# Linear attention in a DiT block: KV per head on 32-column tiles, and KV folded into wo on 32x32 tiles

## The chip, the cores and the metric

The kernel runs on one core of a Trainium2 chip. The metric is the time of one execution on the device in microseconds (us), lower is better. A kernel is timed in several runs beside runs of the kernel before on the same chip. Ratios in this document are the mean time of one kernel's fast runs over the mean time of the other's fast runs of the same rounds, so they are not quite the ratios of the medians that are quoted.

TensorE is the matmul engine. Here a matmul of 128x128 weights with a 128x512 moving operand starts 0.216 us after the one before it. "PE" is TensorE in the profile, "PEld" its weight loads, DVE is VectorE, ACT is ScalarE, POOL is GpSimd, SP issues most DMAs.

## The reference, cut to what matters

```python
h   = layernorm(x) * (1 + ca) + sa                 # x: 2048 x 1024 bf16
q, k, v = split(h @ wqkv)                          # 32 heads of 32 columns
pq, pk  = phi(q), phi(k)
kv  = einsum('bhsd,bhse->bhde', pk, v)             # one 32x32 matrix per head
z   = sum over s of pk
o   = (pq @ kv) / (pq @ z + 1e-6)
x   = x + ga * (o @ wo)
h   = layernorm(x) * (1 + cb) + sb
x   = x + gb * ((silu(h @ w_gate) * (h @ w_up)) @ w_down)     # 3584 wide
```

## The kernel before

The sequence is cut into four chunks (`sc`) of 512 rows. K, V and later Q of a chunk are computed, and `kv_phase` adds the chunk's part to `kv_acc`. At the end KV is folded into `wo`, so that attention costs one matmul with `pq` (`a_ps`). Then the FFN runs per chunk: `gate_up(0), down(0), gate_up(1), down(1), ...`. The `wo_tile` work of the next chunk runs inside `down`.

```python
VW = P + 2
k8 = ctx.enter_context(tc.tile_pool(name="k8", bufs=19))      # 19 buffers of about 8 KB per partition
...
def big(name, shape):                       # every large tile takes one of the 19
    return k8.tile([P] + shape, BF16, name=name, tag="k8")
...
kvs = k8.tile([P, HG * VW + HG * P], F32, name="kvs", tag="k8")
kv_acc = kvs[:, 0:HG * VW].rearrange("p (g e) -> p g e", e=VW)
kvb = kvs[:, HG * VW:].bitcast(BF16).rearrange("p (k g e) -> p k g e", k=2, e=P)
KVZ, KVT = kvb[:, 0], kvb[:, 1]
...
def kv_phase(sc):                           # four heads at once: 128x128, three quarters of it wasted
    for hg0 in range(0, HG, 3):
        nh = min(3, HG - hg0)
        kvp = acc_b("kvp")
        kvv = kvp[:, 0:3 * (P + 1)].rearrange("p (g e) -> p g e", e=P + 1)
        for i in range(nh):
            for t in range(STC):
                mm(kvv[:, i, :], lhsT=pks[sc][:, t, (hg0 + i) * P:(hg0 + i + 1) * P],
                   rhs=vs[sc][:, t, hg0 + i, 0:P + 1], start=(t == 0), stop=(t == STC - 1))
        ... # copied or added to kv_acc on VectorE
...
# after the last chunk: off-diagonal heads are masked away, KV is transposed and folded into wo
KVZ = kv_acc * kvmask                                    # (cut) two VectorE instructions
for hg in range(HG):
    transpose(tpk[:, hg, :], KVZ[:, hg, :])
...
for hg, nb in wf[3 * (qc - 5):3 * (qc - 4)]:             # 16 of these, between Q steps
    mm(ps[:], lhsT=KVT[:, hg, :], rhs=w, start=True, stop=True)
    nc.scalar.copy(out=w, in_=ps[:])
...
def gate_up(sc, between=None):
    for fb in range(NFB):                                # 7 blocks
        for view in (wg_v, wu_v):
            w = big("wgu", [DC, FBW])                    # 1 MB of w_gate, 1 MB of w_up
            nc.sync.dma_start(out=w[:], in_=view[:, :, fb * FBW:(fb + 1) * FBW])
        for fj in range(FPB):                            # 4 groups of 8 gate and 8 up matmuls
            if f % GPT == 0:
                guT[sc].append(big("gu", [min(GPT, FC - f), SCW]))
            ...
```

## Time and profile before

| | before |
|---|---|
| median | 847.77 us (847.76 to 847.96, 3 runs) |
| PE busy | 99% of a span of 846.2 us |
| granted clock of TensorE | 0.999 |

From the page of the kernel before: busy time and share of each engine, then the busy share of TensorE and its granted clock in 40 equal slices (9 is 90% or more).

```profile
PE 838.6 (99%) x4284; PEld 385.7 (46%) x4284; DVE 307.2 (36%) x602; ACT 173.8 (21%) x267; POOL 55.7 (7%) x160
PE   8999999999999999999999999999999999999997
PEclk9999999999999999999999999999999999999999
```

TensorE never waits for long, and its granted clock is 0.999. Whatever is to change the time has to take work from TensorE, or to make it wait.

The chain of waits of the kernel before, in order of time (start in us, length in us, what, number of instructions):

```profile
16.30 5.35 PE acc L98 x24
...
65.16 1.81 PE kvp L98 x32
...
163.92 0.45 PE tp L101 x8
...
168.48 0.65 PE wf L98 x3
...
184.64 14.50 PE a_ps L98 x64
...
289.09 33.78 PE acc L98 x156
322.87 3.45 PE a_ps L98 x16
...
354.81 126.91 PE acc L98 x588
```

A KV phase (`kvp`) costs 1.81 to 1.82 us, four times, and the eight transposes (`tp`) 0.45 us. The fold (`wf`) runs between Q projections: five pieces of three matmuls at 0.65 us and a last one of 0.22 us. The two long `acc` pieces hold `gate_up` and the first matmuls of `down`: no wait interrupts them.

The weights of the FFN come over the SP queue. Three of its DMA issues from the timeline of SP:

```profile
315.13 0.37 SPq L614 DMA_DIRECT2D wd<-in_B_w_down_dram  x1
446.35 0.37 SPq L551 DMA_DIRECT2D wgu<-in_B_w_gate_dram  x1
448.08 0.37 SPq L551 DMA_DIRECT2D wgu<-in_B_w_up_dram  x1
```

These are not free choices of the queue. In `gate_up(1)` the issues are 13.81 us apart in two series, and 13.81 us is one block of 64 matmuls. One series falls on the last use of a block's gate weights, the other, 1.73 us later, on the last use of its up weights. Each load waits for a k8 buffer, and buffers are handed on in program order.

At the start, masks are built on POOL. This is the POOL timeline from 7.5 to 11.5 us:

```profile
8.29 0.31 POOL L181 MEMSET zmask<- 128x256 bf16 x1
8.54 0.58 POOL L184 MEMSET kvmask<- 32x32 bf16 x4
9.15 1.70 POOL L186 MEMSET zmask<- 32x1 bf16 x32
10.94 0.55 POOL L193 TENSOR_TENSOR rstd<-veps,neg_half 128x1 f32<-128x1 f32 x1
```

The third `rstd` could have run at 9.55 us, when its input was ready. It waits behind the memsets.

### The profile page before, as it was taken

How to read it: one execution, taken by the hardware profiler on the slowest of the kernel's cores; microseconds unless marked ns; L12 is line 12 of the kernel's file. 1: busy time of each engine (PE TensorE's matmuls, PEld its weight loads, DVE VectorE, ACT ScalarE, POOL GpSimd, SP SyncE). 2: the span in 40 equal slices, each digit the busy share in tenths (PEclk: the TensorE clock that was granted, in tenths of full speed). 3: DMA queues.
4: the chain of work that ended last, by engine and by line, in shares of the span. 5: the costliest groups of instructions: out<-in, count | busy, mean ns of one | idle time of the engine just before them, and what ended most of it. 6: DMA issues, size and time to landing. Idle time of an engine off the chain costs nothing.

```text
span 846.2 us, 10498 instructions
## 1 busy us (share of the span) xinstructions
PE 838.6 (99%) x4284; PEld 385.7 (46%) x4284; DVE 307.2 (36%) x602; ACT 173.8 (21%) x267; POOL 55.7 (7%) x160
## 2 busy tenths in 40 slices
PE   8999999999999999999999999999999999999997
PEld 4445445544444444444444444444444444444443
DVE  5756464467423325431111344211114431111121
ACT  1455453354311110101111010011110101111000
POOL 2101010012011001100000010000001100000000
PEclk9999999999999999999999999999999999999999
DMA  9893870029976765528434073581604639710011
GB/s 309 301 257 98 243 187 1 1 52 215 348 210 207 214 186 174 181 69 266 146 104 149 19 236 95 159 283 54 199 1 126 185 69 318 240 59 0 19 57 50
DMA packets 125840, 128.74 MB, mean 152 GB/s; under 512 B 33376, under 2 KB 107360, under 8 KB 125280
## 3 DMA queue, kind: packets, MB, share of 16 engines
q1 hardware_dynamic: 122208, 115.36, 46.0%
q0 software_dynamic: 3584, 12.72, 5.0%
q8 instruction: 33, 0.54, 0.3%
q14 instruction: 15, 0.12, 0.0%
HBM read 108.01 MB, written 12.71 MB: 143 GB/s over the span
## 4 chain that ended last, share of the span: by engine, by line
PE 98%; DVE 1%; POOL 0%; DMA 0%; issue 0%; ACT 0%; SPq 0%; DVEq 0%; POOLq 0%
PE acc L98 88%; PE a_ps L98 7%; PE kvp L98 1%; PE modr L98 0%; PE wf L98 0%; DMA x_sb<-in_A_x_dram 0%; DVE stats L199 0%; PE mod_ps L98 0%; PE den L98 0%; POOL zmask L186 0%; PE tp L101 0%; POOL rstd L193 0%; PE bcr L98 0%; DVE e L583 0%; DVE ob L585 0%
## 5 line engine op out<-in xcount | busy, mean ns | idle before, releaser
L98 PE MATMUL acc<-h2T,wgu 128*128 128x512 bf16 x1792 | 387.9, 379 | 0.0
L98 PEld LDWEIGHTS <-wgu 128*128 128x128 bf16 x1792 | 175.1, 98 | 211.0
L98 PE MATMUL acc<-wd,gu 128*128 128x512 bf16 x896 | 196.0, 379 | 0.0
L566 DVE TENSOR_TENSOR gu<-acc,e 128x512 bf16<-128x512 f32 x112 | 77.4, 691 | 300.4 <-PE acc L98 300.4
L565 ACT ACTIVATE e<-acc 128x512 f32<-128x512 f32 x112 | 66.9, 597 | 375.2 <-PE acc L98 375.2
L98 PEld LDWEIGHTS <-gu 128*128 128x128 bf16 x896 | 87.6, 98 | 105.8
L98 PEld LDWEIGHTS <-hT 128*128 128x128 bf16 x512 | 49.6, 98 | 60.8 <-DVE hT L212 1.0
L583 DVE TENSOR_TENSOR e<-acc,gb_bc 128x512 f32<-128x512 f32 x32 | 22.1, 691 | 130.5 <-PE acc L98 130.5
L98 PE MATMUL a_ps<-wo,pq 128*128 128x512 bf16 x256 | 57.9, 379 | 0.6 <-DVE pq L395 0.6
L98 PE MATMUL acc<-hT,wq 128*128 128x512 bf16 x256 | 57.1, 379 | 0.0
L98 PE MATMUL acc<-wk,hT 128*128 128x512 bf16 x256 | 56.9, 379 | 0.0
L98 PE MATMUL acc<-wv,hT 128*128 128x512 bf16 x256 | 55.9, 379 | 0.0
L263 ACT ACTIVATE eb<-acc 128x512 bf16<-128x512 f32 x64 | 37.9, 596 | 62.8 <-PE acc L98 60.5
L209 ACT ACTIVATE xn<-x,nmr,rstd 128x1024 bf16<-128x1024 f32 x16 | 19.8, 1240 | 127.6 <-POOL nmr L207 127.6
L264 DVE TENSOR_SCALAR eb<-eb 128x512 bf16<-128x512 bf16 x64 | 18.4, 291 | 60.6 <-ACT eb L263 60.6
L98 PEld LDWEIGHTS <-pq 128*128 128x128 bf16 x256 | 24.7, 98 | 31.8 <-DVE pq L395 2.6
L98 PEld LDWEIGHTS <-wq 128*128 128x128 bf16 x256 | 24.9, 98 | 29.8
L534 POOL DMA_DIRECT2D x_scratch<-x x16 | 9.6, 600 | 369.6 <-DVE x L527 369.6
L527 DVE TENSOR_TENSOR x<-a_ps,x_sb 128x512 f32<-128x512 f32 x32 | 22.1, 691 | 8.0 <-PE a_ps L98 7.9
L193 POOL TENSOR_TENSOR rstd<-veps,neg_half 128x1 f32<-128x1 f32 x32 | 18.2, 569 | 81.3 <-DVE veps L191 70.4
L301 ACT CAST v<-acc 128x512 bf16<-128x512 f32 x32 | 18.3, 582 | 22.1 <-PE acc L98 22.1
L528 DVE BATCH_NORM_STATS2 stats<-x 128x6 f32<-128x512 f32 x32 | 22.2, 695 | 1.1
(72 smaller groups left out, 280.7 us busy)
## 6 DMA issues: line engine op xcount, KB each, us to landing
wgu<-in_B_w_gate_dram SPq DMA_DIRECT2D x28, 1024.0 KB, 7.4
wgu<-in_B_w_up_dram SPq DMA_DIRECT2D x28, 1024.0 KB, 8.7
x_sb<-in_A_x_dram SPq DMA_DIRECT2D x32, 256.0 KB, 5.9
wml<-in_w_mod_dram SPq DMA_DIRECT2D x8, 1024.0 KB, 8.6
x_scratch<-x POOLq DMA_DIRECT2D x16, 512.0 KB, 3.1
x1r<-x_scratch SPq DMA_DIRECT2D x32, 256.0 KB, 3.0
wd<-in_B_w_down_dram SPq DMA_DIRECT2D x7, 1024.0 KB, 7.7
wme<-in_w_mod_dram SPq DMA_DIRECT2D x4, 1024.0 KB, 11.2
```

What stands on the lines that cost most here:

```text
L98: return tc.keep_in_program_order(nc.tensor.matmul(out, lhsT=lhsT, rhs=rhs, start=start, stop=stop))
L193: nc.gpsimd.tensor_tensor(out=rstd[:, 0:n], in0=veps[:, 0:n], in1=neg_half[:].to_broadcast([P, n]), op=ALU.pow)
L209: nc.scalar.activation(out=dst, in_=src, func=ACT.Identity, bias=nmr[:], scale=rstd[:, 0:1])
L263: nc.scalar.activation(out=e[:], in_=acc, func=ACT.Exp)
L264: nc.vector.tensor_scalar(out=e[:], in0=e[:], scalar1=1.0, scalar2=PHI_EPS, op0=ALU.min, op1=ALU.add)
L301: nc.scalar.copy(out=v[:, t, nb * 4:(nb + 1) * 4, 0:P], in_=acc[:].rearrange("p (g e) -> p g e", e=P))
L527: nc.vector.tensor_tensor(out=x1[:, ns], in0=a_ps[:], in1=x_t[:, ns], op=ALU.add)
L528: nc.vector.bn_stats(out=stats[:, nb, :], in_=x1[:, ns])
L534: nc.gpsimd.dma_start(out=x1_dram[st * P:(st + 1) * P, :], in_=x1[:])
L565: nc.scalar.activation(out=sg[:], in_=ps[0][:], func=ACT.Silu)
L566: gm = nc.vector.tensor_tensor(out=guT[sc][f // GPT][:, f % GPT, :], in0=ps[1][:], in1=sg[:], op=ALU.mult)
L583: nc.vector.tensor_tensor(out=yt[:], in0=y_ps[:], in1=gb_bc[:, ns], op=ALU.mult)
```

## The change

The intent is to stop computing the three quarters of each 128x128 KV product that the head mask throws away. Each head gets its own 32-column tile of the array, four heads side by side, all in one bank of PSUM, the memory that the matmuls of this kernel write to. KV is then compact, so there is no mask; two transposes do in place of eight; the fold runs on sixteen 32x32 tiles, for which the rows of `wo` are regrouped on load. The compact `kv_acc`, `KVB` and `KVT` move to the constant pool, and the k8 pool goes from 19 to 18 buffers.

```diff
-    VW = P + 2
+    VW = HPC * (DH + 1)
-    wo_v = A_wo.rearrange("(c p) n -> p c n", p=P)
+    wo_v = A_wo.rearrange("(h g i e) n -> h g e i n", h=2, g=4, i=HPC)
-    k8 = ctx.enter_context(tc.tile_pool(name="k8", bufs=19))
+    k8 = ctx.enter_context(tc.tile_pool(name="k8", bufs=18))
-    kvs = k8.tile([P, HG * VW + HG * P], F32, name="kvs", tag="k8")
-    ...
+    kv_acc = const.tile([P, HG, DH + 1], F32, name="kv_acc")
+    KVB = const.tile([P, HG, DH], BF16, name="KVB")
+    KVT = const.tile([P, 2, P], BF16, name="KVT")
 ... (kvmask and its memsets go; V is laid out as 33 columns per head, the last one 1.0)
     def kv_phase(sc):
+        W = DH + 1
+        kvp = acc_b("kvp")
+        for hg in range(HG):
+            for t in range(STC):
+                for i in range(HPC):
+                    mm(kvp[i * DH:(i + 1) * DH, hg * W:(hg + 1) * W],
+                       lhsT=pks[sc][:, t, hg * P + i * DH:hg * P + (i + 1) * DH],
+                       rhs=vs[sc][:, t, hg, i * W:(i + 1) * W], start=(t == 0), stop=(t == STC - 1))
 ... (wo is loaded by 8 DMAs of 32 partitions in place of 2 of 128)
+    def fold_wo(h, nb):
+        ns = slice(nb * NB, (nb + 1) * NB)
+        ps = [acc_b("wf") for _ in range(4)]
+        for i in range(HPC):
+            for g in range(4):
+                rs = slice(g * DH, (g + 1) * DH)
+                mm(ps[g][i * DH:(i + 1) * DH, :], lhsT=KVT[rs, h, i * DH:(i + 1) * DH], rhs=wo[h][rs, i, ns],
+                   start=True, stop=True)
+        for g in range(4):
+            (nc.scalar.copy if g % 2 == 0 else nc.vector.tensor_copy)(out=wo[h][:, g, ns], in_=ps[g][:])
+    q_phase(1, 4, 6)
+    fold_wo(0, 0)
+    q_phase(1, 6, 8)
+    fold_wo(0, 1)
+    q_phase(2, 0, 2)
+    fold_wo(1, 0)
+    q_phase(2, 2, 3)
+    fold_wo(1, 1)
```

More of the change, by code (lines that the diff above doesn't have):

```diff
@@ L169 @@
     gb_bc = const.tile([P, D], BF16, name="gb_bc")
-    kvs = k8.tile([P, HG * VW + HG * P], F32, name="kvs", tag="k8")
-    kv_acc = kvs[:, 0:HG * VW].rearrange("p (g e) -> p g e", e=VW)
-    kvb = kvs[:, HG * VW:].bitcast(BF16).rearrange("p (k g e) -> p k g e", k=2, e=P)
-    KVZ, KVT = kvb[:, 0], kvb[:, 1]
+    kv_acc = const.tile([P, HG, DH + 1], F32, name="kv_acc")
+    KVB = const.tile([P, HG, DH], BF16, name="KVB")
+    KVT = const.tile([P, 2, P], BF16, name="KVT")
     Zden = const.tile([P, HG, DH], BF16, name="Zden")
-    kvmask = const.tile([P, P], BF16, name="kvmask")
     zmask = const.tile([P, HG, DH], BF16, name="zmask")
@@ L179, in build_masks @@
     def build_masks():
-        nc.gpsimd.memset(kvmask[:], 0.0)
         nc.gpsimd.memset(zmask[:], 0.0)
@@ L183, in build_masks @@
             rs = slice(h * DH, (h + 1) * DH)
-            nc.gpsimd.memset(kvmask[rs, rs], 1.0)
             for hg in range(HG):
@@ L292, in v_phase @@
         vs[sc] = v
-        nc.gpsimd.memset(v[:, :, :, P:VW], 1.0)
+        vh = v.rearrange("p t g (i e) -> p t (g i) e", e=DH + 1)
+        nc.gpsimd.memset(vh[:, :, :, DH:DH + 1], 1.0)
         for t in range(STC):
@@ L300, in v_phase @@
                                      start=(cc == 0), stop=(cc == DC - 1))
-                nc.scalar.copy(out=v[:, t, nb * 4:(nb + 1) * 4, 0:P], in_=acc[:].rearrange("p (g e) -> p g e", e=P))
+                nc.scalar.copy(out=vh[:, t, nb * 16:(nb + 1) * 16, 0:DH], in_=acc[:].rearrange("p (h e) -> p h e", e=DH))
     def q_phase(sc, lo=0, hi=DC):
@@ L313, in kv_phase @@
     def kv_phase(sc):
-        for hg0 in range(0, HG, 3):
-            nh = min(3, HG - hg0)
-            kvp = acc_b("kvp")
-            kvv = kvp[:, 0:3 * (P + 1)].rearrange("p (g e) -> p g e", e=P + 1)
-            for i in range(nh):
-                for t in range(STC):
-                    mm(kvv[:, i, :], lhsT=pks[sc][:, t, (hg0 + i) * P:(hg0 + i + 1) * P],
-                                     rhs=vs[sc][:, t, hg0 + i, 0:P + 1], start=(t == 0), stop=(t == STC - 1))
-            dst = kv_acc[:, hg0:hg0 + nh, 0:P + 1]
-            if sc == 0:
-                nc.vector.tensor_copy(out=dst, in_=kvv[:, 0:nh, :])
-            else:
-                nc.vector.tensor_tensor(out=dst, in0=dst, in1=kvv[:, 0:nh, :], op=ALU.add)
+        W = DH + 1
[6 more added lines that the diff above has]
+                       rhs=vs[sc][:, t, hg, i * W:(i + 1) * W], start=(t == 0), stop=(t == STC - 1))
+        kvv = kvp[:, 0:HG * W].rearrange("p (g e) -> p g e", e=W)
+        if sc == 0:
+            nc.vector.tensor_copy(out=kv_acc[:], in_=kvv)
+        else:
+            nc.vector.tensor_tensor(out=kv_acc[:], in0=kv_acc[:], in1=kvv, op=ALU.add)
     def mod_load(cols):
@@ L477 @@
         if sc == 2:
-            wo = load_w(wo_v, 0, "wo")
+            wo = [big("wo", [4, D]) for _ in range(2)]
+            for h in range(2):
+                for g in range(4):
+                    nc.sync.dma_start(out=wo[h][g * DH:(g + 1) * DH, :, :], in_=wo_v[h, g])
             for cc in range(DC):
@@ L484 @@
     kv_phase(NSC - 1)
-    for h in range(2):
-        hs = slice(4 * h, 4 * h + 4)
-        nc.vector.tensor_tensor(out=KVZ[:, hs, :], in0=kv_acc[:, hs, 0:P],
-                                in1=kvmask[:].unsqueeze(1).to_broadcast([P, 4, P]), op=ALU.mult)
-        nc.vector.tensor_tensor(out=Zden[:, hs, :], in0=kv_acc[:, hs, P:P + 1].to_broadcast([P, 4, DH]),
-                                in1=zmask[:, hs, :], op=ALU.mult)
-    q_phase(1, 2, 4)
-    tpk = acc_b("tp", (HG, P), BF16)
-    for hg in range(HG):
-        transpose(tpk[:, hg, :], KVZ[:, hg, :])
-    nc.scalar.copy(out=KVT[:, 0:4, :], in_=tpk[:, 0:4, :])
-    nc.vector.tensor_copy(out=KVT[:, 4:8, :], in_=tpk[:, 4:8, :])
-    den_norm(0)
-    q_phase(1, 4, 5)
-    wf = [(hg, nb) for hg in range(HG) for nb in range(NNB)]
-    for qc in range(5, 11):
-        q_phase(1 + qc // 8, qc % 8, qc % 8 + 1)
-        for hg, nb in wf[3 * (qc - 5):3 * (qc - 4)]:
-            ps = acc_b("wf")
-            w = wo[hg // 4][:, hg % 4, nb * NB:(nb + 1) * NB]
-            mm(ps[:], lhsT=KVT[:, hg, :], rhs=w, start=True, stop=True)
-            nc.scalar.copy(out=w, in_=ps[:])
+    nc.vector.tensor_copy(out=KVB[:], in_=kv_acc[:, :, 0:DH])
+    nc.vector.tensor_tensor(out=Zden[:], in0=kv_acc[:, :, DH:DH + 1].to_broadcast([P, HG, DH]),
+                            in1=zmask[:], op=ALU.mult)
+    q_phase(1, 2, 4)
+    tpk = acc_b("tp", (2, P), BF16)
+    for h in range(2):
+        transpose(tpk[:, h, :], KVB[:, 4 * h:4 * h + 4, :].rearrange("p g e -> p (g e)"))
+    nc.vector.tensor_copy(out=KVT[:], in_=tpk[:])
+    den_norm(0)
+    def fold_wo(h, nb):
[6 more added lines that the diff above has]
+                   start=True, stop=True)
+        for g in range(4):
+            (nc.scalar.copy if g % 2 == 0 else nc.vector.tensor_copy)(out=wo[h][:, g, ns], in_=ps[g][:])
[7 more added lines that the diff above has]
+    fold_wo(1, 1)
     h2Ts = {}
```

## The prediction

> **What bounds it now.** TensorE. The page has PE busy 99% of 846.2 us at clock 0.999; in the chain of work PE is 98%. So only TensorE time, or a new TensorE wait, moves the total.
>
> **What the change takes from TensorE** (durations: chain and timeline of before)
> - KV: 4 x 1.82 us (32 matmuls, 128x129 moving, 57 ns apart). After: 128 matmuls per phase, 33 columns, four column tiles. The denominator matmuls show such tiles: four start 3.4 ns apart, then the next four 56 ns later (N=128). With N=1 on the whole array starts are 25 ns apart[...]. If that floor holds per tile and not per instruction: 32 steps x 25 ns = 0.8 us. Entering and leaving a tile shape costs about 0.1 us each way here (gap 0.15 us for 0.056 around the denominator)[...]. With some loss to instruction supply (256 instructions in under 1 us, never seen here) I take 1.2 us: -2.5 us in four phases.
> - Fold: 16 matmuls x 0.216 = 3.45 us become 4 groups of 16 on 32x32 tiles, each 0.22 + 0.05 + 0.2 of drains = 0.47 us: -1.6 us; the last group, one q step after the third, may wait some 0.5 us for its four banks. Net -1.1 us.
> - Transposes 8 to 2: -0.34 us.
> - Start: the chain runs through kvmask memsets on POOL (0.6 us between 8.5 and 9.1 us) that hold back an rstd: -0.5 us.
> Sum -4.5 us. The smaller DVE masks and evictions, the strided V evictions and the eight smaller wo loads are off the chain.
>
> **What it adds: one k8 buffer less in the FFN.** kvs was one of 19 buffers and came free after the fold; now there are 18 for good. In the timeline of DMA issues every weight load of gate_up(0) and gate_up(1) is issued when a buffer is released, in program order. By that count, moved by one buffer:
> - The last w_down load now goes out at 315.13 us and lands at 320.19; TensorE needs it at 316.8 + 24 x 0.216 = 321.9. One buffer later it goes out at 316.8, and second loads 1.7 us after another take 6.8 to 7.7 us: lands near 324, wait about 2 us at the start of down(0).
> - gate_up(1) (two pq and wo still alive) has 6 buffers for w_gate, w_up and gu instead of 7. The up weights of blocks 5 and 6 then go out only when the gate weights of the block before come free, 3.46 us before they are needed; such a load takes 5.2 to 5.6 us. Two waits of about 2 us.
> Later sections hold fewer pq, so nothing there. Sum +6 us; I count 5 for doubt.
>
> **Prediction:** 847.8 - 4.5 + 5 = 848.3 us, range 843.0 to 853.0. Faster by over 2%: 0.01; within 2%: 0.97; slower: 0.02.
>
> **What would show it.** KV phases of 0.8 to 1.4 us in the chain (3.2 us would mean that the 25 ns floor is per instruction); fold groups near 0.5 us; up to the FFN the kernel is 4 to 5 us ahead; then new idle time of PE "acc" released by DMA wd and wgu, about 2 us each, once at the start of down(0), twice late in gate_up(1).
>
> **What would make it wrong.** Instruction supply limiting KV; 32x32 tiles not running side by side (fold as long as before); the scheduler giving buffers in another order, so that the waits vanish (then about 843) or multiply; a late wo load holding DVE and with it the phi evictions.

The 25 ns are read from the one-column matmuls of the kernel before, which mostly start 25 ns apart, and the "0.2 of drains" is two changes of tile shape at the 0.1 us each read around its denominator. That both carry over to the small tiles, and that tiles run side by side in the fold, were my estimates.

## More of the kernel before

`a_ps` at 184.64 us is the first output tile of attention, so everything before it is projections, KV and fold.

## The result

The changed kernel took 853.35 us (median of 4 runs, 852.19 to 853.73) against 847.84 us (4 runs) for the kernel before. The ratio of the fast runs is 1.0059, with a 95% interval from 1.0045 to 1.0073: slower by 0.6%, and within 2%. The change does remove TensorE work, and the kernel still gets slower.

The chain of waits of the changed kernel, same columns as above:

```profile
65.25 1.13 PE kvp L98 x128
...
126.71 1.51 PE modr L98 x26
128.22 1.26 issue
129.48 0.61 PE modr L98 x6
...
162.91 0.11 PE tp L101 x2
...
167.14 0.36 PE wf L98 x16
...
182.53 14.50 PE a_ps L98 x64
...
314.75 7.09 DMA wd<-in_B_w_down_dram
...
322.90 3.45 PE a_ps L98 x16
...
354.84 91.53 PE acc L98 x424
...
446.39 5.23 DMA wgu<-in_B_w_up_dram
...
462.23 5.33 DMA wgu<-in_B_w_up_dram
467.61 19.99 PE acc L98 x84
487.60 3.45 PE a_ps L98 x16
```

Read it against the chain of before at three points. `a_ps` of the first tile starts at 182.53 us in place of 184.64: the kernel is 2.11 us ahead. The next `a_ps` starts at 322.90 in place of 322.87: the lead is gone, and a `wd` load now stands in the chain. The piece of `gate_up(1)` and its first `down` output, which ran from 354.81 for 126.91 us, now takes from 354.84 to 487.60, 132.76 us: 5.85 us are lost there, and two loads of `w_up` stand in the chain.

The waits view gives the idle time of TensorE that each load ended (us in total, times, longest):

```profile
PE acc L98 <- DMA wgu<-in_B_w_up_dram: 3.8, 2, 2.0
PE acc L98 <- DMA wd<-in_B_w_down_dram: 2.0, 1, 2.0
PE modr L98 <- issue: 1.3, 1, 1.3
```

The view counts from the modelled end of the previous matmul. Counted from start to start, less the usual 0.216 us, the three FFN waits are 2.15, 2.01 and 2.12 us.

The SP timeline has the loads on which they hang:

```profile
446.39 0.37 SPq L558 DMA_DIRECT2D wgu<-in_B_w_up_dram  x1
448.12 0.37 SPq L558 DMA_DIRECT2D wgu<-in_B_w_gate_dram  x1
```

The event that released a gate load before (446.35) now releases an up load (446.39). The load order has slipped by one buffer.

A third loss is in the clock. Here are the two stretches of the changed kernel after the second wait, from a table of windows: bounds and length in us, busy time and number of instructions of PE, PEld, DVE, ACT and POOL, granted clock, DMA share, GB/s.

```profile
467.61:471.10 3.49, 3.49 (x9) 1.31 (x10) 0.00 (x0) 0.00 (x0) 0.00 (x0) 0.51 0.56 204
471.10:487.60 16.50, 16.50 (x78) 7.43 (x77) 2.77 (x4) 1.79 (x3) 0.00 (x0) 1.00 0.00 1
```

The clock records hold one stretch of 0.50 that begins at 467.68 us, when the second wait ends, and lasts 3.41 us. Its matmuls start 0.427 us apart in place of 0.216, so it costs about 1.7 us.

The small tiles do bring what they are for: in the chain a KV phase takes 1.13 us for 1.81 before, with four times the matmuls, and a fold group of 16 takes 0.36 us. In the records of one KV phase the matmuls come in steps of four, one for each tile. In the first eight steps the four start about 3.4 ns apart, and from the second to the eighth the steps are 25 ns apart. From the tenth on the steps are 33 ns apart and the four are spread evenly over them, about 8 ns from one to the next. All four KV phases show the same pattern. The first eight steps, with their weight loads, are 64 instructions. From the tenth on 8 instructions take 33 ns, or 4.2 ns each. What changes the pace there no run here isolates.

And the POOL timeline at the start:

```profile
8.17 1.42 POOL L182 MEMSET zmask<- 32x1 bf16 x32
9.66 0.63 POOL L189 TENSOR_TENSOR rstd<-veps,neg_half 128x1 f32<-128x1 f32 x1
```

The third `rstd` runs 1.28 us earlier (9.66 for 10.94).

### The profile page after: what moved, and what is told of

Read it like the earlier page. It is cut to its first block, busy times and chain, and to the rows that moved or that the text cites. A ratio compares the mean times of both kernels' runs of the same rounds, so it can differ in the third digit from the quotient of the medians.

```text
span 851.7 us, 11341 instructions
## 1 busy us (share of the span) xinstructions
PE 838.1 (98%) x4710; PEld 382.0 (45%) x4710; DVE 307.5 (36%) x600; ACT 169.6 (20%) x258; POOL 57.0 (7%) x155
## 4 chain that ended last, share of the span: by engine, by line
PE 96%; DMA 2%; DVE 1%; issue 0%; ACT 0%; DVEq 0%
PE acc L98 88%; PE a_ps L98 7%; DMA wgu<-in_B_w_up_dram 1%; DMA wd<-in_B_w_down_dram 1%; PE kvp L98 1%; PE modr L98 0%; PE mod_ps L98 0%; PE den L98 0%; PE tp L101 0%; ACT eb L259 0%; DVE wo L504 0%; PE wf L98 0%; PE bcr L98 0%; DVE pq L262 0%; DVE e L590 0%
```

## The experiments

All outputs are right. "e2" and the like are the labels of the runs.

### e1: only the buffer is taken away

```diff
-    k8 = ctx.enter_context(tc.tile_pool(name="k8", bufs=19))
+    k8 = ctx.enter_context(tc.tile_pool(name="k8", bufs=18))
-    kvs = k8.tile([P, HG * VW + HG * P], F32, name="kvs", tag="k8")
+    kvs = const.tile([P, HG * VW + HG * P], F32, name="kvs")
```

Everything else is the kernel before.

> The kernel before, with only the buffer taken away: kvs moves to the constant pool and k8 has 18 buffers; KV, masks and fold as before. Buffer theory: the same three TensorE waits as after the change (w_down at the start of down(0), about 2.1 us; w_up in blocks 5 and 6 of gate_up(1), about 2.0 us each), and perhaps 1.7 us of half clock after the last: 847.8 + 6.1 to 7.9 = 853.9 to 855.7 us. Rival (the small tiles or the schedule that came with them upset the loads): no waits, 847.8 us.

It took 855.30 us (854.21 to 857.31, 4 runs) against 848.01 (9 runs), ratio 1.0087 (1.0072 to 1.0101). The waits view shows the same three waits:

```profile
PE acc L98 <- DMA wgu<-in_B_w_up_dram: 3.6, 2, 1.9
PE acc L98 <- DMA wd<-in_B_w_down_dram: 2.5, 1, 2.5
```

With KV, masks and fold untouched, one buffer less makes these waits. The small tiles have no part in them. In its profiled run the clock was not halved, though the waits were there.

### e2: the change with the buffer given back

To make room for the 19th buffer, `kv_acc`, `KVB` and `KVT` share one k8 tile that comes free after the fold, and three small tiles get one buffer in place of two.

```diff
-    k8 = ctx.enter_context(tc.tile_pool(name="k8", bufs=18))
+    k8 = ctx.enter_context(tc.tile_pool(name="k8", bufs=19))
-    kv_acc = const.tile(...); KVB = const.tile(...); KVT = const.tile(...)
+    KW = HG * (DH + 1)
+    kvs = k8.tile([P, KW + 2 * P], F32, name="kvs", tag="k8")
+    kv_acc = kvs[:, 0:KW].rearrange("p (g e) -> p g e", e=DH + 1)
+    KVB = kvs[:, KW:KW + P].bitcast(BF16)...; KVT = kvs[:, KW + P:KW + 2 * P].bitcast(BF16)...
-    x1r bufs=2, dsum bufs=2, rb bufs=2
+    x1r bufs=1, dsum bufs=1, rb bufs=1
```

> The change with the buffer given back: kv_acc, KVB and KVT share one k8 tile that comes free after the fold, k8 has 19 buffers again, paid for by one x1r buffer for two and one dsum and rb for two. Buffer theory: no wait on wd or wgu, clock up throughout, and the 2.1 us gained before the FFN stays: 847.8 - 2.1 = 845.7 us (845.2 to 846.2). Rival: the waits remain, about 853.

It took 845.96 us (845.43 to 847.70, 5 runs) against 848.01, ratio 0.9979 (0.9966 to 0.9993). The chain has its two long pieces back:

```profile
286.71 33.77 PE acc L98 x156
...
352.43 126.91 PE acc L98 x588
```

They are as long as before the change (33.78 and 126.91 us), and no load stands in the chain of the FFN. Together e1 and e2 settle the point: the loss is the buffer, in both directions.

### e4 and e8: where TensorE waited for nothing that the profile shows

The 1.3 us of "issue" among the modulation rows (`modr`) after the third KV phase is also in e2, where it is 1.70 us. TensorE's instructions come as packets of 16 KB here (queue q8, 16,384 bytes each in the trace of the changed kernel): the page counts 37 of them for the changed kernel and 33 for the kernel before, with 9,420 and 8,568 instructions of PE and PEld. That is about 256 for each packet. The new KV phase alone has 256. In e4 the modulation rows move away from the KV phase:

```diff
             kv_phase(sc - 1)
-            if sc >= 2:
-                row = mod_rows(blks)
             k_phase(sc, 2, 4)
+            if sc >= 2:
+                row = mod_rows(blks)
+            k_phase(sc, 4, 6)
             ... (mod_bc, mod_cols)
-            k_phase(sc, 4, 8)
+            k_phase(sc, 6, 8)
```

> The change with 19 buffers (e2), and the modulation rows moved behind two more K groups, so that they no longer follow the 256 KV instructions at once. Instruction-supply theory: the 1.3 to 1.9 us in which TensorE waited for nothing that the profile shows, among the modulation rows after the third KV phase, is gone; two more changes of tile shape cost 0.2 us; a_ps of the first output tile starts 1.1 to 1.6 us earlier than in e2 (182.3 us). Rival (the modulation rows wait for their weights or a semaphore): the wait is still there or shorter only by the 3.5 us moved.

It took 844.63 us (843.52 to 846.39, 4 runs), ratio 0.9960 (0.9945 to 0.9975). The wait is gone, as the timeline of PE shows for the third phase (start, length, instructions; an idle time would stand in brackets):

```profile
127.06 1.20 PE L98 MATMUL kvp<-v,pk 128*32 128x33 bf16 x128
128.19 3.63 PE L98 MATMUL acc<-wk,hT 128*128 128x512 bf16 x15
131.75 1.91 PE L98 MATMUL modr<-wml,sc 128*32 128x512 bf16 x32
```

From the first KV phase to `a_ps` e4 needs 116.12 us and e2 117.78, 1.66 us less. The start of `a_ps` itself, which I had named, was later (182.65 us), because e4's profiled run had half clock from 25.06 us on, again for 3.41 us. That is a point where the expectation was stated badly: a difference inside the program should be taken between two points of it. e4 alone does not exclude its rival, since data that came 1.7 us late for the modulation rows would also have been there 3.6 us later. e8 does.

e8 moves nothing, but pushes the stream of instructions by 80 before the second KV phase:

```diff
             k_phase(sc, 0, 2)
+            if sc == 2:
+                pad = acc_b("pad")
+                for _ in range(40):
+                    mm(pad[:, 0:1], lhsT=sel[:, 0, :], rhs=sel[:, 0, 0:1], start=True, stop=True)
             kv_phase(sc - 1)
```

> e2 with 40 useless one-column matmuls (80 instructions with their weight loads, 40 x 25 ns = 1.0 us) just before the second KV phase. TensorE's instructions come in blocks of 256, one 16 KB packet each. Block theory: [...] From the stall in e2 a block starts 52 instructions into the third KV phase, so 124 into the second. With 80 more: one starts 44 into the second and the next 300, which is among its modulation rows: a stall of 1.3 to 1.9 us appears there, where e2 has none; in the third KV phase a block starts 28 before and the next 228 into it: about 0.9 us of stall inside that KV phase, and none among the modulation rows after it. Rival (the third modulation rows wait for data): no stall at the second, the same stall at the third.

The 0.9 us were my estimate.

It took 846.07 us (845.88 to 846.70, 4 runs), ratio 0.9976 (0.9962 to 0.9990). The timeline of PE at the second KV phase:

```profile
94.73 1.20 PE L98 MATMUL kvp<-v,pk 128*32 128x33 bf16 x128
95.75 1.47 PE L98 MATMUL modr<-wml,sc 128*32 128x512 bf16 x22
98.38 0.82 PE L98 MATMUL modr<-wml,sc 128*32 128x512 bf16 x10 [1.15 <-issue]
```

A wait appears where there was none, after 256 KV instructions and 22 matmuls with their 22 loads: 300 instructions, the number stated in advance. The wait at the third phase is gone. So the wait belongs to the block of instructions and not to the data of the modulation rows. The landing times say the same: the last weights of these rows (`wml`) landed at 67.80 us in e8, 29 us before the new wait, and at 106.88 us in the changed kernel, 21 us before its wait at the third phase. The other half of the expectation failed: no 0.9 us wait inside the third KV phase (1.13 us, as ever). The packet for that block started at 123.80 us, 4.0 us before the KV phase; my reckoning was wrong: the 28 instructions before the KV phase are 14 matmuls, or 3.0 us and not 1.7, and the packet had started even earlier than that.

In the stalled cases the packet moved from 126.99 to 127.99 us in the changed kernel and TensorE went on at 129.48, and from 95.78 to 96.91 us in e8 and it went on at 98.38. From the start of the packet to the next instruction that is 2.5 to 2.6 us (2.4 to 2.6 in all seven profiles with this wait: the changed kernel twice, e2, e3, e5, e8 and e9).

### e5: the fold groups further apart

```diff
-    q_phase(1, 4, 6);  fold_wo(0, 0);  q_phase(1, 6, 8);  fold_wo(0, 1)
-    q_phase(2, 0, 2);  fold_wo(1, 0);  q_phase(2, 2, 3);  fold_wo(1, 1)
+    q_phase(1, 4, 5);  fold_wo(0, 0);  q_phase(1, 5, 7);  fold_wo(0, 1)
+    q_phase(1, 7, 8);  q_phase(2, 0, 1);  fold_wo(1, 0);  q_phase(2, 1, 3);  fold_wo(1, 1)
```

In the changed kernel the timeline of PE at the last two groups was:

```profile
174.92 0.43 PE L98 MATMUL wf<-wo,KVT 32*32 32x512 bf16 x16
175.29 1.90 PE L98 MATMUL acc<-hT,wq 128*128 128x512 bf16 x8
177.12 0.58 PE L98 MATMUL wf<-wo,KVT 32*32 32x512 bf16 x3
177.93 0.43 PE L98 MATMUL wf<-wo,KVT 32*32 32x512 bf16 x13 [0.23 <-DVE wo L504]
```

A q step is eight matmuls of a Q projection. The last group stands for 0.2 us before its third matmul and for 0.6 us before its fourth, from start to start, until VectorE has evicted (copied out) the bank that the fourth one writes.

> The change with 19 buffers (e2), and the four fold groups each two q steps apart, in place of one q step before the last. Theory: the fourth group waited 0.6 to 0.8 us because its banks were still being evicted behind the phi work on VectorE; with two steps it does not wait, each group costs 0.47 us with its shape changes, and a_ps starts 0.8 us earlier than in e2, near 181.5 us. Rival (the wait is the price of the 32x32 shape): still 0.6 us before the fourth group.

It took 844.90 us (844.48 to 845.01, 4 runs), ratio 0.9961 (0.9946 to 0.9977). The same place:

```profile
172.86 0.43 PE L98 MATMUL wf<-wo,kvs 32*32 32x512 bf16 x16
173.23 3.63 PE L98 MATMUL acc<-hT,wq 128*128 128x512 bf16 x16
176.78 0.43 PE L98 MATMUL wf<-wo,kvs 32*32 32x512 bf16 x16
```

All 16 matmuls run through. From the first KV phase to `a_ps` it needs 116.93 us for 117.78 in e2, 0.85 us less, and `a_ps` starts at 181.39 us.

### e6: all three mended

> 19 buffers, modulation rows later and folds spaced. If the three causes add up: e2 (845.96 us) - 1.3 - 0.8 = about 843.9 us (843.2 to 844.8), 4 us faster than the kernel before, no wait on wd or wgu and no stall at modr or wf.

e6 is e2 with the edits of e4 and e5. It took 844.40 us (843.48 to 844.96, 5 runs) against 848.01 (9 runs), ratio 0.9954 (0.9941 to 0.9966). From the first KV phase to `a_ps` it needs 115.31 us: 2.47 less than e2, where 1.66 and 0.85 add up to 2.51. This version beats both kernels, the one before by 0.5% and the change as given by about 1% (medians of 844.40 and 853.35 us, from runs on different chips).

### e3, e9 and a repeat: the half clock

In the changed kernel's profiled run the clock fell to half after the second wait of `gate_up(1)`. The theory was that the idle time does that. To test it, e3 fills the two waits of `gate_up(1)` with useless matmuls. Cut from its expectation is the wording of this theory; the 1.7 us in it are the cost of the 3.41 us of half clock in the profiled run.

```diff
                 for w in wb:
+                    if sc == 1 and fb in (5, 6) and fj == 0 and ps:
+                        keep_warm(acc_b("warm"), 8)
                     acc = acc_a()
```

> The changed kernel with eight useless 128x128x512 matmuls (8 x 0.216 = 1.73 us) put into each of the two waits of gate_up(1), between the first gate and the first up group of blocks 5 and 6. Clock theory [...]: no half clock in the trace after start and 853.35 - 1.7 = 851.6 us, although there are 16 matmuls more. Rival (the half clock has another cause, or falls elsewhere): 853.3 us or more, half clock still there.

It took 854.70 us (853.10 to 855.65, 5 runs), ratio 1.0075 (1.0062 to 1.0088). The gain of 1.7 us did not come. The profiled run had no half clock after the start, but neither had that of e1, which has the waits unfilled. And mean clocks of single runs went from 0.996 to 0.999, so in some of them the clock fell somewhere that the one profile doesn't show. This settled nothing. e9 fills the wait at the start of `down(0)` as well (nine matmuls before the last four of the first output), and the changed kernel ran again beside it.

> The changed kernel once more, as the neighbour of e9 on one chip. Expected: 852 to 855 us; the fastest run near 852.2 us with a mean clock of 1.0, slower runs with a lower mean clock.

> The changed kernel with useless matmuls in all three waits of the FFN: nine before the last four w_down steps of the first output, eight in each of the two waits of gate_up(1). e3 filled two of three and its runs still showed mean clocks of 0.996 to 0.999, so it settled nothing. Clock theory (idle time of TensorE in these waits brings the half clock in some runs): runs of e9 cluster at the fastest time of the changed kernel beside it, mean clock 0.999 to 1.0, median about 1.2 us lower. Rival (the half clock comes at random or elsewhere): the same spread of times and clocks in both.

| run | us and mean clock of its runs |
|---|---|
| changed kernel again | 851.67 (0.999), 851.82 (0.999), 852.69 (1.0), 856.02 (0.995), 857.81 (0.993), 858.61 (0.993) |
| e9 | 851.80 (0.999), 851.96 (1.0), 852.92 (0.999), 853.27 (0.999), 853.74 (0.997) |
| before, same chip | 847.69 to 850.12, clocks 0.998 to 1.0 (11 runs) |

The medians are 854.36 and 852.92 us, the ratios to before 1.0076 (1.0051 to 1.0102) and 1.0052 (1.0039 to 1.0065). Their intervals overlap. The fastest runs are the same, although e9 has 25 matmuls more, about 5.4 us of them: they really sat in the waits. The slow runs with clocks of 0.993 to 0.995 are missing in e9. That is what the idle theory expects, but with five and six runs it is a hint and not a proof, and one run of e9 still had 0.997. That slow runs are runs with a low clock is shown. They were not profiled, so what brought the clock down in them is not seen.

The length of a wait alone does not tell either. In the changed kernel's profiled run the half clock followed a wait of 2.0 us by the waits view; in that of e1 the wait at the start of `down(0)` was 2.5 us by the same view, and no half clock came. What brings the clock down was not shown.

## Why the prediction was right or wrong, point by point

The mechanism was right, and every wait that was forecast stood where it had been said. One more wait and a stretch of half clock were not in the sum. The sum was 5 us too low: 848.3 us predicted, 853.35 measured. The median is 0.35 us over the upper end of the range; 1.0059 times 847.84 is 852.8, just inside. Terms are those of the profiled run, taken between points of the two chains.

| step of the prediction | predicted | measured |
|---|---|---|
| four KV phases | -2.5 us | -2.7 us |
| transposes | -0.34 | -0.34 |
| fold, net of the last group's wait | -1.1 | -0.8 |
| start | -0.5 | +0.1 |
| instruction supply after KV | named as a risk, not in the sum | +1.6 |
| sum up to `a_ps` | -4.5 | -2.1 |
| three waits in the FFN | +6, counted as 5 | +6.3 |
| half clock after the waits | absent | +1.7 |

The measured terms add up to 5.9 us, and the chain's last TensorE piece ends 5.88 us later (847.62 for 841.74 us at the same place).

- **KV, right.** A phase is 1.13 us in the chain; I had taken 1.2. The 25 ns from start to start that the one-column matmuls show in the kernel before are found here per 32-column tile: in the first eight steps four tiles start within about 10 ns, and from the second to the eighth a step takes 25 ns. Two of the four phases are followed by modulation rows of the same tile shape and so save one change of shape, which gives -0.78 us there for -0.59.
- **Changes of tile shape, right.** A fold group costs 0.46 us from the last plain matmul to the next, with both changes, for 0.47 predicted. At such a change the start of a matmul comes 0.309 us after that of the one before, for 0.216: 0.09 us.
- **The last fold group's wait, undersized.** I said some 0.5 us; it cost 0.8 us against the other groups. e5 removed 0.85 us.
- **Start, right on average and wrong in this run.** `rstd` came earlier, as said. But the first K matmul stands behind the warm-up matmuls, and in the profiles its start went with the moment at which the full clock was granted. In the nine profiles without the masks it started between 15.58 and 16.39 us (median 15.82) for 16.27 and 16.30 in the two with them: -0.46 us by the medians. Where the full clock came between 4.58 and 5.43 us it was 15.58 to 15.67 us; where it came at 6.83 and 6.88 us (e9, the changed kernel) it was 16.37 and 16.39. In the profiled run of the changed kernel the full clock came last of all, at 6.88 us, and the gain was gone.
- **Instruction supply, misjudged.** I had looked for it inside the KV phase, where steps only stretch from 25 to 33 ns, for a reason that no run isolates. The wait came behind it, among the 64 instructions that followed at once: 1.26 us of "issue" after the third KV phase, ended 2.5 us after a packet began; after the second KV phase the same 64 ran through. e4 and e8 show that it goes with the stream of instructions. This was 1.6 us that the sum lacked.
- **The buffer, right.** The three loads, the events that release them and waits of about 2 us were all as said: 2.15, 2.01 and 2.12. The discount from 6 to 5 "for doubt" was not earned.
- **The half clock, missed.** The prediction had TensorE idle for 2 us and priced it at 2 us. In the profiled run the second of two such waits, with 13.8 us between them, was followed by 3.41 us of half clock. What brings it was not shown: the profiles of the repeat and of e1 had such waits and no half clock. The fastest run of the changed kernel had a mean clock of 1.0 and took 852.19 us, 4.4 us over the fastest of before; without the half clock the terms above add up to 4.2.

With the instruction supply, the half clock and the full 6 us for the waits the sum would have read 848.3 + 1 + 1.6 + 1.7 = 852.6 us.

## What to carry to other kernels

A change that frees TensorE time can be paid with the memory it moves (here 2.1 us gained up to `a_ps`, 6.3 us of waits in the FFN): count who holds each buffer of a shared pool over the whole program, and which load is released by which last use, before giving one away. Packing narrow matmuls side by side did here what it is meant to do (a KV phase of 1.13 us for 1.81), but it turned 32 matmuls into 128 short ones: the 256 instructions of a KV phase with 64 more at once behind them stood still for 1.26 us in one place of the changed kernel and not in another, and with two K groups put between them (e4) the wait was gone. And look at the time between two uses of a set of PSUM banks: one q step behind the third, the fourth fold group lost 0.8 us to the eviction on VectorE; two q steps behind it (e5) it ran through.
